# An mLSTM cell with a two-layer MLP: first-chunk gates loaded once and copied by TensorE, later masks by affine selections

## The chip, the cores and the metric

The kernel runs on one core of a Trainium2 chip. A core has five engines with queues of their own: TensorE (PE; its weight loads are shown as PEld), VectorE (DVE), ScalarE (ACT), GpSimd (POOL) and SyncE (SP), and 16 DMA engines that serve the loads and stores that the queues issue. Here SyncE and ScalarE issue them. The metric is the device time of one launch in microseconds, as the median of several runs; the time before is 476.22 us (three runs, 475.19 to 476.83).

## The reference

Four batches, eight heads, 768 steps, head dimension 40. Each step of the cell updates a matrix state `C` and a vector state `n` with stabilized gates; the result goes through a MLP with a leaky ReLU.

```python
for t in range(S):
    m_new = np.maximum(f[t] + m, i[t])
    f_stab = np.exp(f[t] + m - m_new)
    i_stab = np.exp(i[t] - m_new)
    m = m_new
    C = f_stab * C + i_stab * outer(v[t], k[t])
    n = f_stab * n + i_stab * k[t]
    y[t] = sigmoid(o[t]) * (C @ q[t]) / np.maximum(abs(n @ q[t]), 1.0)
...
x = y.transpose(0, 2, 1, 3).reshape(3072, 320)
h = x @ w_in            # 320 x 2048
out = np.maximum(0.01 * h, h) @ w_out   # 2048 x 320
```

The gates `i` and `f` are one number for each batch, head and step: 32 rows (batch times head) of 768.

## The kernel before

**Tiling.** The 768 steps are cut into six chunks of 128. A "step" `s` of the program is one batch of one chunk, `c, b = divmod(s, 4)`, so there are 24 of them. Within a chunk the cell is computed in parallel form: scores of keys and queries, multiplied by a matrix of exponentials of gate differences with a causal mask, times the values; the state is carried from chunk to chunk. Chunk 0 works on whole 128x128 score matrices; the later chunks use halves of 64. The MLP of a chunk (`ff_units`) is interleaved with the cell of the next one.

**Order.** The program order on TensorE, VectorE, ScalarE and GpSimd is written out by hand (`first_chunk`, then a loop over chunks); loads issued through `sync` or `by_act` keep their program order by the class `Ordered` (line 96 is the line of all SyncE issues). The weights come as 64-bit words and are turned into 32-bit floats on the chip by `narrow_weights` (two ScalarE and four VectorE instructions for each piece, lines 300 to 309).

**Gates of chunk 0.** Lines 109 to 111 load the first 128 columns of both gates four times each, into the four groups of 32 partitions of `f0` and `i0` (`RG` = 4), the forget gates by ScalarE's queue and the input gates by SyncE's. `gates(0)` then runs two scans and two subtractions on all 128 partitions (lines 325 to 333), which leaves `a` and `bu[:, 0]` four times. `a` lies in a corner of the buffer `acts` called `early`, beside the bf16 copies of the identity and of the causal mask. `gates(c)` for later chunks works on 32 partitions. `load_fi` loads the gates of later chunks; for chunks 1 and 2 ScalarE's queue issues them.

**The spread.** The matrix of exponents for a batch and head is mask[t', t] + bu[t'] + a[t]. `spread_masks` puts the mask into four PSUM banks by bf16 products (line 479). `spread_first` (line 495) adds the two others by products with a contraction of 32: one with a broadcast column of the identity as weights and `a` as moving operand, one the other way round with `bu`. The four products of a group of heads stand in the four groups of 32 rows, `rows = ts(r, BH)`, so TensorE can hold them side by side; this is what the four copies are for. `first_exps` (line 504, ScalarE) takes the exponentials for steps 0 and 1. A second spread, of `a` alone, serves steps 2 and 3.

**First-chunk order.** `first_chunk` (line 1169) issues the loads of steps 0 and 1 (keys, queries, values, then output gates), the first weights, then the gates, six products `warm(6)` whose result is never used (line 367), the mask products, the spread, the transposes of the gates (`gates_T`, lines 373 and 380), `prep_vu(0)` on GpSimd (lines 540 and 544), the exponentials, then `u_transpose(0)` (line 635: four transposes of the keys and four of the queries; the copies out of PSUM, line 638, are VectorE's here) and `u_scores(0)` (line 649 on TensorE, product with the exponentials on VectorE in line 653).

**Later masks.** In chunks 1 to 5, `spread(s)` or `feed_slowly` broadcasts `a` from a DRAM buffer into a tile `w` of 128 partitions x 8 heads x 64; partitions 0 to 63 and 64 to 127 hold the two halves of the chunk. `prep_mask` (line 522, GpSimd) adds `cm2`, the 64x64 causal mask in both halves of the partitions, which `prepare_tiles` copied into `i0` (line 176). `prep_exp` (line 530, ScalarE) takes the exponentials. `prep_mask` runs on GpSimd in one queue with `split_v` (line 413, values into their halves), the scaled state (line 684), the scaled keys (line 550) and others.

Of the kernel before, what the change touches and what calls it, by code (L numbers as in the profile page):

```python
# [8 lines left out]

F32 = mybir.dt.float32  # L10
# [4 lines left out]
ALU = mybir.AluOpType  # L15
# [4 lines left out]
def kernel(  # L20
# [26 lines left out]
    nc = tc.nc  # L47
    B, H, S, D = q.shape
    P = 128
    BH = B * H  # L50
# [11 lines left out]
    SL = P // 2  # L62
# [4 lines left out]
    GT = B * P  # L67
# [13 lines left out]
    wk = ctx.enter_context(tc.tile_pool(name="wk", bufs=2))  # L81
    psf = ctx.enter_context(tc.tile_pool(name="psf", bufs=4, space=PSUM))
    psc = ctx.enter_context(tc.tile_pool(name="psc", bufs=4, space=PSUM))
# [22 lines left out]
    i_all = i_gate.rearrange("b h s -> (b h) s")  # L106
    f0 = gp.tile([P, P], F32, name="f0")
    i0 = gp.tile([P, P], F32, name="i0")
    for r in range(RG):
        nc.scalar.dma_start(f0[ts(r, BH), :], f_all[:, :P])  # L110
        sync.dma_start(i0[ts(r, BH), :], i_all[:, :P])
    fi = {}

    def load_fi(c):
# [5 lines left out]
    load_fi(1)  # L120

    ident = consts.tile([P, P], F32, name="ident")
    make_identity(nc, ident[:])
    zeros = consts.tile([P, 1], F32, name="zeros")
    nc.vector.memset(zeros[:], 0.0)

# [4 lines left out]
        cmask[:], cmask[:], compare_op=ALU.is_ge, fill=-1e30,  # L131
        base=0, pattern=[[1, P]], channel_multiplier=-1,
    )
    cm2 = i0[:, :SL]

    NL = 4
# [8 lines left out]
    w_all = consts.tile([P, NL, H * P], F32, name="w")  # L147
    acts = consts.tile([P, NF, GT], F32, name="acts")
    acts_l = acts[:].rearrange("p f t -> p (f t)")
    early = acts_l[:, 5 * GT : 5 * GT + 3 * P].rearrange("p (n t) -> p n t", t=P)  # L150
    identb, cmaskb = (early[:, n, : P // 2].bitcast(BF16) for n in range(2))
    nc.gpsimd.tensor_copy(identb, ident[:])
    nc.gpsimd.tensor_copy(cmaskb, cmask[:])
    for n in range(NL):
        nc.vector.memset(kn[:, n, :, D:], 0.0)
        nc.vector.memset(qn[:, n, :, D:], 0.0)
        nc.gpsimd.memset(S_t[n][:, 1, :, D:], 2.0)
        nc.gpsimd.memset(S_t[n][SL:, 0], 0.0)
# [13 lines left out]

    def prepare_tiles():

        for u in range(2):
            nc.gpsimd.tensor_copy(cm2[ts(u, SL)], cmask[ts(u, SL), ts(u, SL)])
        nc.gpsimd.memset(xb[:], 0.0)
        for t in rb_t:
            nc.gpsimd.memset(t[:, :, RL:], 0.0)
# [138 lines left out]
    def gates(c):  # L318


        m0 = m0s.get(c)
        n = P if c == 0 else BH
        fc, il = (f0[:], i0[:]) if c == 0 else (fi[c][:, 0, :], fi[c][:, 1, :])
        F = wk.tile([n, P], F32, name="F", bufs=1)
        nc.vector.tensor_tensor_scan(F[:], fc, zeros[:n].to_broadcast([n, P]), 0.0, op0=ALU.add, op1=ALU.add)
        if c > 0:
            nc.vector.tensor_scalar(il, il, scalar1=m0[:], scalar2=None, op0=ALU.subtract)
        m = wk.tile([n, P], F32, name="m", bufs=1)
        nc.vector.tensor_tensor_scan(m[:], fc, il, -1e30 if c == 0 else 0.0, op0=ALU.add, op1=ALU.max)
        a = early[:, 2, :] if c == 0 else wk.tile([n, P], F32, name="a", bufs=1)  # L330
        nc.vector.tensor_tensor(a[:], F[:], m[:], op=ALU.subtract)
        bu = wk.tile([n, 3, P], F32, name="bu", bufs=1)
        nc.vector.tensor_tensor(bu[:, 0, :], il, F[:], op=ALU.subtract)
        if c + 1 < NB:
            m1 = wk.tile([BH, 1], F32, name="m0")
            if c == 0:
                nc.vector.tensor_copy(m1[:], m[:BH, P - 1 :])
            else:
                nc.vector.tensor_tensor(m1[:], m0[:], m[:, P - 1 :], op=ALU.add)
            m0s[c + 1] = m1  # L340
        if c > 0:
            na = wk.tile([BH, 1], F32, name="na")
            nc.vector.tensor_tensor(na[:], m[:, SL - 1 : SL], F[:, SL - 1 : SL], op=ALU.subtract)
        bus[c] = bu, a, (na if c > 0 else None)
# [19 lines left out]
    def warm(n):  # L364
        t = psf.tile([P, P], F32, name="warm", tag="mm")
        for _ in range(n):
            nc.tensor.matmul(t[:], lhsT=ident[:], rhs=ident[:], start=True, stop=True)
# [97 lines left out]
    def spread_q(s):  # L465
# [4 lines left out]
        for r in range(2):  # L470
            sync.dma_start(
                d["ea"][ts(r, SL)], a_dr[c, 1, 1 - r, b * H : (b + 1) * H, :].partition_broadcast(SL),
            )

    def spread_masks():

        ab = [psf.tile([P, 2, H // RG, P], F32, name=f"ab{r}", tag="mm") for r in range(RG)]
        for t in ab:
            nc.tensor.matmul(
                t[:].rearrange("p n m t -> p (n m) t"), lhsT=identb,  # L480
                rhs=cmaskb.unsqueeze(1).to_broadcast([P, 2 * H // RG, P]), start=True, stop=False, skip_group_check=True,
            )
        return ab

    def spread_first(ab, a, bu, s2):

        for n in range(2):
            st.setdefault(s2 + n, {})["w"] = w_all[:, s2 + n].rearrange("p (h t) -> p h t", t=P)
            for m in range(H // RG):
                for left in (False, True)[: 1 if bu is None else 2]:  # L490
                    for r in range(RG):
                        bh = (s2 + n) * H + m * RG + r
                        rows = ts(r, BH)
                        pick = ident[rows, r * BH + bh : r * BH + bh + 1].to_broadcast([BH, P])
                        nc.tensor.matmul(
                            ab[r][:, n, m, :], lhsT=bu[rows, 0, :] if left else pick, rhs=pick if left else a[rows, :],
                            start=False, stop=left or bu is None, skip_group_check=True,
                        )

# [17 lines left out]
    def prep_mask(s):  # L517
        if s in masked:
            return
        masked.add(s)  # L520
        w = st[s]["w"]
        nc.gpsimd.tensor_tensor(w, w, cm2.unsqueeze(1).to_broadcast([P, H, SL]), op=ALU.add)  # L522

    def prep_exp(s):

# [103 lines left out]
    def u_transpose(s, copies):  # L629
        d = st[s]  # L630
        d["kqT"] = wk.tile([P, 2, PR * P], F32, name="kqT")
        for i in range(2):
            tp = psc.tile([P, PR, P], F32, name="tkq", tag="c")
            for j in range(PR):
                nc.tensor.transpose(
                    tp[:, j, :], d["kq"[i]][:, 2 * j : 2 * j + 2, :].rearrange("p h d -> p (h d)"), ident[:],
                )
            copies[i](d["kqT"][:, i], tp[:].rearrange("p j t -> p (j t)"))
# [530 lines left out]
    def first_chunk():  # L1169

        for n in range(2):
            for i in range(3):
                load_first(n, i)
        for n in range(2):
            load_first(n, 3)
        load_weights(0, (0,))
        on_v, on_s = nc.vector.tensor_copy, nc.scalar.copy
        gates(0)
        gates_exp(0)
        load_fi(2)  # L1180
        warm(6)
        ab = spread_masks()
        bu, a, _ = bus[0]
        spread_first(ab, a, bu, 0)
        gates_T(0, bu)
        prep_vu(0)
        first_exps(ab, 0)
        u_transpose(0, (on_v, on_v))
        u_scores(0)
        u_transpose(1, (on_s, on_s))  # L1190
        ab = spread_masks()
        gates(1)
        u_scores(1)
        prep_vu(1)
        prepare_tiles()
        e = next_exps(ab, 2)
        w, w1 = narrow_weights(0, 0), narrow_weights(0, 1)
        n0, n1 = narrow_weights(1, 0), narrow_weights(1, 1)
        ffs = []
        prep_o(0)  # L1200
        prep_o(1)
        u_values(0)
        gate(0)
        spread_first(ab, a, None, 2)
        u_values(1)
        load_first(2, 0)
        load_first(2, 1)
        load_weights(0, (1,))
        load_first(3, 0)
        load_first(3, 1)  # L1210
        load_first(2, 2)
        load_first(3, 2)
        load_first(2, 3)
        load_first(3, 3)
        load_weights(1, (0,))
        load_weights(1, (1,))
        run(e, 6)
        u_x(0)
        gate(1)
        run(w, 2)  # L1220
        run(w, 4)
        u_x(1)
        state(0)
        state(1)
        state_copy(0)
        state_copy(1)
        prepare_step(0)
        prepare_step(1)
        run(e, 2)
        ffs = ff_units(0)  # L1230
        u_transpose(2, (on_s, on_s))
        run(e, 4)
        gates_exp(1)
        run(w1, 2)
        run(e, 4)
        ffs[0]()
        run(w1, 2)
        prep_vu(2)
        prep_vu(3)
        u_scores(2)  # L1240
        u_transpose(3, (on_v, on_s))
        run(w1, 2)
        u_gates(1)
        u_scores(3)
        prep_o(2)
        prep_o(3)
        u_values(2)
        ffs[1]()
        gate(2)
        u_values(3)  # L1250
        gate(3)
        u_x(2)
        state(2)
        u_x(3)
        state(3)
        state_copy(2)
        run(n0, 4)
        state_copy(3)
        run(n0, 2)
        run(n1, 6)  # L1260
        prepare_step(2)
        prepare_step(3)
        return ffs
# [160 lines left out]
```

## Time and profile before

| What | Value |
|---|---|
| median of three runs | 476.22 us |
| lowest and highest run | 475.19 and 476.83 us |
| span of the profiled execution | 472.6 us |
| TensorE busy | 462.6 us (98%) |
| TensorE weight loads busy | 417.8 us (88%) |
| VectorE busy | 339.1 us (72%) |
| ScalarE busy | 203.7 us (43%) |
| GpSimd busy | 172.0 us (36%) |
| mean granted TensorE clock | 0.999 |
| HBM traffic over the span | 124 GB/s |

The profile is one execution. The span runs from its first instruction to its last; the time of a run also holds what lies around the span. The views used below are: the chain of work that ended last, followed back from the end (the shares of the span that each engine or line holds in it; "SPq" is SyncE's queue issuing transfers); busy time by windows (for each engine the busy time and the number of instructions, then the granted clock, the busy share of the DMA engines and GB/s); the timeline (start, duration, engine, line, operation, tiles and shapes, a count where like instructions are merged, and in square brackets the idle time before it with what ended it); and the groups of instructions (busy time, mean ns of one, idle before). An f32 product of TensorE appears as two entries in the counts, a transpose as one.

### The profile page before, as it was taken

The numbers are of one execution on the slowest core, as the hardware profiler recorded it, in microseconds if no ns is written. First come the engines' busy times: TensorE is split into PE (matmuls) and PEld (weight loads), VectorE is DVE, ScalarE is ACT, GpSimd is POOL, SyncE is SP. The second block draws the span as 40 slices with busy tenths as digits, with TensorE's granted clock in tenths as the row PEclk, the third lists the DMA queues.
The fourth block names the chain that finished last, engine by engine and source line by source line (L and its number), as shares of the span: only waits on it lengthen the run. The fifth ranks groups of instructions, "written<-read, shape, count | busy, mean of one in ns | idle before, by whom it ended". The sixth has DMA issues, their size and how long they took to land.

```text
span 472.6 us, 14150 instructions
## 1 busy us (share of the span) xinstructions
PE 462.6 (98%) x5729; PEld 417.8 (88%) x5729; DVE 339.1 (72%) x607; ACT 203.7 (43%) x497; POOL 172.0 (36%) x205
## 2 busy tenths in 40 slices
PE   7998999999999999999999999999999999999997
PEld 6787878777788899988999988999988999988997
DVE  3878589999579989878688867788947786105531
ACT  3755888755336511367311366311456311253210
POOL 4340577264335164923214923214822005300020
PEclk9999999999999999999999999999999999999999
DMA  9999988877742594865755764853875203100001
GB/s 117 174 176 183 223 192 229 199 154 159 155 135 56 157 171 107 185 152 115 179 125 108 172 144 120 196 120 76 189 147 122 65 21 81 58 0 2 8 8 42
DMA packets 161281, 59.31 MB, mean 126 GB/s; under 512 B 123904, under 2 KB 152640, under 8 KB 161216
## 3 DMA queue, kind: packets, MB, share of 16 engines
q1 hardware_dynamic: 121088, 51.20, 49.0%
q10 hardware_dynamic: 40128, 7.21, 9.3%
q8 instruction: 45, 0.74, 0.7%
q14 instruction: 20, 0.16, 0.2%
HBM read 51.68 MB, written 6.70 MB: 124 GB/s over the span
## 4 chain that ended last, share of the span: by engine, by line
PE 86%; SPq 6%; DMA 3%; DVE 1%; ACT 1%; issue 1%; POOL 0%; DVEq 0%; ACTq 0%
PE ph L1021 33%; PE po L914 33%; PE po L879 8%; SPq L96 6%; PE pT L796 3%; PE sd L708 3%; PE ph L857 3%; DMA acts<-in_moe_w_in_dram 2%; DMA acts<-in_v_dram 1%; PE sd L714 1%; PE hN L768 1%; PE tk L621 0%; ACT kqT L627 0%; PE tq L606 0%; DVE w_in L308 0%
## 5 line engine op out<-in xcount | busy, mean ns | idle before, releaser
L914 PE MATMUL po<-w_out,acts 128*128 128x160 f32 x640 | 89.1, 300 | 0.0
L914 PEld LDWEIGHTS po<-w_out,acts 128*128 128x128 f32 x640 | 87.3, 190 | 0.6 <-ACT acts L1046 0.3
L1021 PE MATMUL ph<-xT,w_in 64*128 64x256 f32 x720 | 82.7, 378 | 0.0
L1021 PEld LDWEIGHTS ph<-xT,w_in 64*128 64x128 f32 x720 | 69.5, 187 | 8.3 <-issue 0.6
L1050 DVE TENSOR_TENSOR acts<-acts,ph 128x512 f32<-128x512 f32 x60 | 38.4, 682 | 40.4 <-PE ph L1021 40.3
L914 PE MATMUL po<-raw,acts 128*128 128x160 f32 x480 | 66.4, 300 | 0.0
L914 PEld LDWEIGHTS po<-raw,acts 128*128 128x128 f32 x480 | 65.4, 190 | 0.3
L1054 ACT COPY acts<-ph 128x512 f32<-128x512 f32 x60 | 32.2, 588 | 49.5 <-PE ph L1021 49.5
L522 POOL TENSOR_TENSOR w<-w,i 128x512 f32<-128x512 f32 x20 | 31.9, 1603 | 53.2 <-DMA w<-a_dr 22.1
L1046 ACT ACTIVATE acts<-acts 128x1024 f32<-128x1024 f32 x30 | 31.6, 1055 | 40.6 <-DVE acts L1050 32.3
L684 POOL TENSOR_TENSOR S<-S,f 40x336 f32<-40x336 f32 x36 | 31.3, 868 | 46.7 <-PE pT L796 31.1
L530 ACT ACTIVATE w<-w,gT 128x64 f32<-128x64 f32 x160 | 41.6, 337 | 12.3 <-DMA a_dr<-a 5.3
L725 DVE TENSOR_TENSOR qn<-w,sd 64x384 f32<-64x384 f32 (+1 forms) x80 | 33.4, 418 | 13.7 <-ACT acts L1054 7.8
L857 PE MATMUL ph<-xT,w_in 64*128 64x256 f32 x320 | 37.9, 383 | 1.8 <-DVE w_in L309 0.7
L879 PE MATMUL po<-w_out,acts 128*128 128x320 f32 x128 | 36.7, 437 | 0.0
L857 PEld LDWEIGHTS ph<-xT,w_in 64*128 64x128 f32 x320 | 31.5, 187 | 5.8 <-ACT acts L865 1.1
L810 POOL TENSOR_TENSOR xb<-xb,den 128x320 f32<-128x320 f32 x16 | 11.6, 727 | 67.7 <-DVE xb L807 65.4
L1021 PE MATMUL ph<-acts,w 64*128 64x256 f32 x320 | 36.3, 379 | 0.0
L1021 PEld LDWEIGHTS ph<-acts,w 64*128 64x128 f32 x320 | 30.6, 187 | 3.6
L879 PEld LDWEIGHTS po<-w_out,acts 128*128 128x128 f32 x128 | 23.5, 190 | 9.2 <-ACT acts L865 0.3
L595 DVE TENSOR_TENSOR qn<-kqT,ea 64x512 f32<-64x512 f32 x32 | 30.9, 965 | 0.8
L952 POOL TENSOR_TENSOR y<-y,raw 128x160 f32<-128x160 f32 x10 | 9.5, 953 | 59.2 <-ACT y L951 59.2
(181 smaller groups left out, 736.5 us busy)
## 6 DMA issues: line engine op xcount, KB each, us to landing
rb<-in_k_dram SPq DMA_DIRECT2D x64, 80.0 KB
rb<-in_q_dram SPq DMA_DIRECT2D x64, 80.0 KB
rb<-in_o_gate_dram SPq DMA_DIRECT2D x64, 80.0 KB
ea<-a_dr SPq DMA_DIRECT2D x32, 128.0 KB
raw<-in_moe_w_out_dram SPq DMA_DIRECT2D x6, 640.0 KB
w<-a_dr ACTq DMA_DIRECT2D x24, 128.0 KB
x_dr<-x SPq DMA_DIRECT2D x64, 40.0 KB
xT<-x_dr SPq DMA_DIRECT2D x16, 160.0 KB
```

The lines of the kernel that those rows point to most:

```text
L522: nc.gpsimd.tensor_tensor(w, w, cm2.unsqueeze(1).to_broadcast([P, H, SL]), op=ALU.add)
L530: yield nc.scalar.activation(w[:, h, :], w[:, h, :], AF.Exp, bias=gT[c][:, 0, bh : bh + 1], scale=1.0)
L595: nc.vector.tensor_tensor(mixed(s)[rows, 1 - r], d["kqT"][rows, 1].rearrange("p (h t) -> p h t", t=SL), d["ea"][rows], op=ALU.mult,)
L684: nc.gpsimd.tensor_tensor(new, old, g, op=ALU.mult)
L725: nc.vector.tensor_tensor(mixed(s)[toks, u, hs], w[toks, hs], bank[1 - u][to[u][hs.start], hs], op=ALU.mult,)
L857: nc.tensor.matmul(ph[r][:, cols], lhsT=w_row(r, slot, j), rhs=xT[DP * r : DP * (r + 1), slot, cols], start=(slot == 0), stop=(slot == KC ...
L879: nc.tensor.matmul(po[n][:], lhsT=acts[:, f, ts(n, P)], rhs=w_out[:, f, :], start=(f == 0), stop=(f == NF - 1),)
L914: nc.tensor.matmul(bank[:], lhsT=left[:, f, :], rhs=right[:, f, :], start=f == 0, stop=f == KH - 1)
L1021: nc.tensor.matmul(bank[r][:, e, :], lhsT=left(r)[rows, e], rhs=right(r)[rows], start=first and e == 0 and m == 0, stop=e == 1 and m == le ...
L1046: nc.scalar.activation(to, z, AF.Prelu, alpha=0.01)
L1050: nc.vector.tensor_tensor(to[:, 2 * r : 2 * r + 2], to[:, 2 * r : 2 * r + 2], bank[r], op=ALU.add)
L1054: nc.scalar.copy(to[:, 2 * r : 2 * r + 2], bank[r])
```

## The change

- Each gate of chunk 0 is loaded once, into 32 partitions; `gates(0)` works on 32 partitions, with `a` in a tile of its own.
- A new function `replicate` makes the four copies: a matrix of 32 x 128 that holds the 32x32 identity four times (`early[:BH, 2]`, written by GpSimd) is the weight of two products with `a` and `bu[:, 0]`; VectorE copies the result of 128 x 256 from PSUM to `early`. `spread_first` takes its operands from there.
- `u_transpose(0)` is moved ahead of `spread_first`, behind `replicate`.
- `warm(6)` becomes `warm(2)`.
- The identity is built by a memset and two selections of 64x64 on its diagonal, instead of `make_identity`, which was a memset and one selection of 128x128.
- `prep_mask` no longer adds a mask tile: two affine selections on GpSimd, one for each half of the partitions, fill -1e30 where the column is before the row. `cm2` and the two copies that built it are gone.

```diff
-    for r in range(RG):
-        nc.scalar.dma_start(f0[ts(r, BH), :], f_all[:, :P])
-        sync.dma_start(i0[ts(r, BH), :], i_all[:, :P])
+    nc.scalar.dma_start(f0[:BH], f_all[:, :P])
+    sync.dma_start(i0[:BH], i_all[:, :P])
...
-    make_identity(nc, ident[:])
+    nc.gpsimd.memset(ident[:], 0.0)
+    for u in range(2):
+        part = ident[ts(u, SL), ts(u, SL)]
+        nc.gpsimd.affine_select(
+            part, part, compare_op=ALU.not_equal, fill=1.0, base=0, pattern=[[-1, SL]], channel_multiplier=1,
+        )
...
-    cm2 = i0[:, :SL]
...
-    early = acts_l[:, 5 * GT : 5 * GT + 3 * P].rearrange("p (n t) -> p n t", t=P)
+    early = acts_l[:, 5 * GT : 6 * GT].rearrange("p (n t) -> p n t", t=P)
...
+    nc.gpsimd.tensor_copy(early[:BH, 2, :].rearrange("p (r n) -> p r n", r=RG), ident[:BH, :BH].unsqueeze(1).to_broadcast([BH, RG, BH]))
...
-        for u in range(2):
-            nc.gpsimd.tensor_copy(cm2[ts(u, SL)], cmask[ts(u, SL), ts(u, SL)])
...
-        n = P if c == 0 else BH
-        fc, il = (f0[:], i0[:]) if c == 0 else (fi[c][:, 0, :], fi[c][:, 1, :])
+        n = BH
+        fc, il = (f0[:BH], i0[:BH]) if c == 0 else (fi[c][:, 0, :], fi[c][:, 1, :])
...
-        a = early[:, 2, :] if c == 0 else wk.tile([n, P], F32, name="a", bufs=1)
+        a = wk.tile([n, P], F32, name="a", bufs=1)
...
+    def replicate(a, bu):
+
+        rows = early[:, 2:]
+        t = psc.tile([P, 2, P], F32, name="rep", tag="c")
+        pick = rows[:BH, 0, :]
+        for n, part in enumerate((a[:], bu[:, 0, :])):
+            nc.tensor.matmul(t[:, n, :], lhsT=pick, rhs=part, start=True, stop=True)
+        nc.vector.tensor_copy(rows, t[:])
+        return rows[:, 0, :], rows[:, 1, :]
...
-        nc.gpsimd.tensor_tensor(w, w, cm2.unsqueeze(1).to_broadcast([P, H, SL]), op=ALU.add)
+        for u in range(2):
+            part = w[ts(u, SL)]
+            nc.gpsimd.affine_select(
+                part, part, compare_op=ALU.is_ge, fill=-1e30, base=0, pattern=[[0, H], [1, SL]], channel_multiplier=-1,
+            )
...
-        warm(6)
+        warm(2)
         ab = spread_masks()
         bu, a, _ = bus[0]
-        spread_first(ab, a, bu, 0)
+        a, left = replicate(a, bu)
+        u_transpose(0, (on_v, on_v))
+        spread_first(ab, a, left, 0)
         gates_T(0, bu)
         prep_vu(0)
         first_exps(ab, 0)
-        u_transpose(0, (on_v, on_v))
         u_scores(0)
```

More of the change, by code (lines that the diff above doesn't have):

```diff
@@ L6 @@
 from concourse.bass import ts
-from concourse.masks import make_identity
 from concourse._compat import with_exitstack
@@ L336, in gates @@
             if c == 0:
-                nc.vector.tensor_copy(m1[:], m[:BH, P - 1 :])
+                nc.vector.tensor_copy(m1[:], m[:, P - 1 :])
             else:
@@ L495, in spread_first @@
                         nc.tensor.matmul(
-                            ab[r][:, n, m, :], lhsT=bu[rows, 0, :] if left else pick, rhs=pick if left else a[rows, :],
+                            ab[r][:, n, m, :], lhsT=bu[rows, :] if left else pick, rhs=pick if left else a[rows, :],
                             start=False, stop=left or bu is None, skip_group_check=True,
```

## The prediction

> **What bounds the kernel.** I read the shares of the chain first, then busy time by window, then the timeline of the first 20 us and of 36 to 72 us, and last who waited for whom there.
>
> ```profile
> PE 86%; SPq 6%; DMA 3%; DVE 1%; ACT 1%; issue 1%; POOL 0%; DVEq 0%; ACTq 0%
> ...
> 126.00:200.00 74.00, 74.00 (x1040) 69.21 (x1040) 61.35 (x101) 27.58 (x71) 38.99 (x35) 1.00 0.62 135
> ```
>
> The second line is a stretch of 74 us in which TensorE is busy for 74.00. The windows from 70 to 400 us are all like it, so nothing that shortens VectorE or GpSimd work there can shorten the run. TensorE is busy 462.6 of 472.6 us; most of the 10 us that are open lie before 70 us, and before 52 us the chain is not TensorE's. It is SyncE's row of DMA issues, unbroken from 0.75 to 28.96 us, then a transfer of 8.66 us:
>
> ```profile
> 28.96 8.66 DMA acts<-in_moe_w_in_dram
> ...
> 37.73 0.80 ACT w_in L300
> ```
>
> So the run is a head paced by transfers, behind which about 400 us of full TensorE lie. What the head gains or loses by 70 us appears at the end nearly whole.
>
> ```profile
> 0.75 1.79 SPq L96 DMA_DIRECT2D i<-in_i_gate_dram  x4
> 0.76 1.84 ACTq L110 DMA_DIRECT2D f<-in_f_gate_dram  x4
> 2.58 0.42 SPq L96 DMA_DIRECT2D kn<-in_k_dram  x1
> 4.03 0.42 DVE L325 TENSOR_TENSOR_SCAN F<-f,zeros 128x128 f32<-128x128 f32 x1 [1.47 <-DMA f<-in_f_gate_dram]
> 6.03 0.81 PE L495 MATMUL ab<-acts,ident 32*128 32x128 f32 x8
> 8.43 0.39 PE L495 MATMUL ab<-ident,bu 32*128 32x128 f32 x8
> 8.83 0.66 PE L635 MATMUL tkq<-ident,kn 128*128 128x128 f32 x4
> 10.87 1.16 PE L649 MATMUL sc<-kqT 40*128 40x128 f32 x16 [0.94 <-DVE kqT L638]
> 12.13 1.28 DVE L653 TENSOR_TENSOR w<-w,sc 128x512 f32<-128x512 f32 x2 [1.32 <-PE sc L649]
> ```
>
> Four issues on each queue come ahead of everything else. The scan of the gates waits for the last f piece, and the keys cannot be asked for before 2.58.
>
> ```profile
> 3.00:4.00 1.00, 1.00 (x7) 1.00 (x7) 0.00 (x0) 0.33 (x1) 0.89 (x3) 1.00 0.38 71
> 4.00:5.00 1.00, 1.00 (x4) 0.43 (x4) 0.94 (x3) 0.95 (x1) 0.89 (x3) 1.00 1.09 199
> ```
>
> The last two columns are the busy share of the transfer engines and GB/s: 0.38 and 71 in the fourth microsecond, 1.09 and 199 in the fifth. Until the keys are asked for the engines are mostly empty; afterwards they are behind, since the same kind of 160 KB load takes 0.42 us to issue at 2.58 but 1.16 at 5.19.
>
> **Three loads fewer on each queue.** Four issues on SyncE take 1.79 plus the gap to 2.58, so 0.46 each. Three fewer bring the keys and all loads behind them 1.38 us forward (2.58 to 1.20). The bytes that vanish (6 x 16 KB = 98 KB) moved while the engines were mostly idle, and I count nothing for them. The Trainium skill, DMA: Bandwidth & Descriptors, section "Issuing engines are not separate DMA queues", says that the time a sequencer takes to initiate a transfer is usually small relative to the transfer. By that rule only bytes would count, an estimate of 98 KB at the 180 GB/s of the later windows, 0.5 us; the row at 71 GB/s speaks for the issue time here.
>
> The stream keeps the 1.38 us as long as it stays behind. The signs that it does, up to 63 us:
>
> ```profile
> 37.73 0.79 ACT L300 ACTIVATE w_in<-acts 128x640 f32<-128x640 f32 x1 [0.37 <-DMA acts<-in_moe_w_in_dram]
> ...
> 45.42 0.80 ACT L300 ACTIVATE w_in<-raw 128x640 f32<-128x640 f32 x1 [2.17 <-DMA raw<-in_moe_w_in_dram]
> ...
> 46.05 0.25 PE L621 MATMUL tk<-ident,kn 64*40 64x64 f32 x2 [1.07 <-DMA kn<-in_k_dram]
> ...
> 60.93 1.79 POOL L522 TENSOR_TENSOR w<-w,i 128x512 f32<-128x512 f32 x1 [7.27 <-DMA w<-a_dr]
> 62.97 0.95 POOL L413 COPY S<-acts 64x320 f32<-64x320 f32 x2 [0.24 <-DMA acts<-in_v_dram]
> ...
> 69.64 0.23 PE L714 MATMUL sd<-S,vu 64*40 64x42 f32 x1 [0.96 <-POOL vu L550]
> ```
>
> At each of them the last wait ends with a transfer or with GpSimd work right behind one. For the whole shift to reach 37.73, compute must be earlier by about 1.0 (1.38 less the 0.37 that ScalarE idled); at 45.42 ScalarE has 2.17 to spare, and the transfer alone decides.
>
> **The compute of the head.** The scan now starts 1.43 us after the last f issue ends (2.60 to 4.03). One issue ends at 1.22, so it starts at 2.65; the memsets of VectorE end at 2.56 and do not hold it. Its five instructions take 1.32 (4.03 to 5.35) and end at 3.97, 1.38 earlier.
>
> GpSimd ahead of TensorE: one 128x128 selection (0.29) becomes two of 64x64. None of that size is in the trace; a 64x64 copy is 0.23 and the whole selection 0.29, so I take 0.27 each, +0.25. The bf16 masks are ready at 2.4 instead of 2.13. The copy of the picks (at most the 0.29 of a 128x128 copy) ends at 2.7. GpSimd's queue behind it, eight memsets ending at 5.58, moves by 0.5; its next work comes at 9.41, so nobody waits.
>
> TensorE: warm products go from 12 entries to 4, at 0.22 each 1.7 to 2.6. The mask products (4.19 to 6.03, 1.84) then run 2.6 to 4.45. The two copying products stand in the same 32 rows and cannot lie side by side as a group of eight L495 entries does in 0.41; 2 x 0.41 gives 5.3. The VectorE copy of 128x256 lies between 0.22 (128x64, L380) and 0.65 (128x512, L638): 0.38, ready at 5.75. Meanwhile the eight transposes of step 0 run: 1.1 us at the fast pace (8.83 to 9.93), twice that at the slow one; I take 1.7, to 7.0. They need q of step 0. By the bytes per microsecond the first 480 KB were in by 5.7, and 1.38 earlier with a microsecond to land is 5.3, when only k is being transposed; if q came 1 us later, the spread would too.
>
> The spread's eight groups take 0.41 each at the start and 0.22 from 7.5 on: 1.8 at best, 3.3 at worst. From 7.0 with the pace rising as before: 8.9. Exponentials start 9.2 instead of 8.85, 0.35 later. But the scores of step 0 no longer wait for the copies of kqT (VectorE makes these from 6.2 to 7.7, ahead of its copy of gT): they end by 10.3 instead of 12.03. The product L653 then waits for the exponentials, 11.3 for its second half, and ends at 11.95 against 13.41. Compute gains 1.4 (0.2 with the slow pace throughout, 1.8 with the fast one), enough for the 1.0 above. The transposes of step 1 and the copies that fill kqT on ScalarE move by as much.
>
> **Masks.** Twenty sums of 128x512 become forty selections of 64x512; the two 64x64 copies that made the mask (0.52, at 12.80) go.
>
> ```profile
> 1.37 0.29 POOL L130 TENSOR_SCALAR_AFFINE_SELECT cmask<-cmask 128x128 f32<-128x128 f32 x1
> ...
> 2.39 0.52 POOL L158 MEMSET S<- 64x512 f32 x1
> ...
> L522 POOL TENSOR_TENSOR w<-w,i 128x512 f32<-128x512 f32 x20 | 31.9, 1603 | 53.2 <-DMA w<-a_dr 22.1
> ```
>
> No selection of 512 columns is in the trace. From below: the memset's slope, (0.52 - 0.20)/384 = 0.83 ns per column, on 0.29 gives 0.61. From above: four times 0.29 is 1.16. A pair is 1.2 to 2.3 against 1.60. A selection has one input like the memset, so I take 1.3. From 70 us on TensorE covers either end. Before, two places can feel it. The first mask (48.77 to 50.49) ends just ahead of the exponentials at 51.12, after a gap of 0.43 on ScalarE, whose L865 releases TensorE at 52.41 (idle 0.73): 0.3 gained, or 0.6 lost. The second ends at 62.72, 0.24 ahead of a transfer: nothing gained, or 0.5 lost before the GpSimd chain that TensorE awaits at 69.64. The transfer behind the second takes back most of what the first gains: I count 0.05, with -0.6 and +0.7 as ends.
>
> **Sum.** 1.38 + 0.05 = 1.4 us. Span 472.6 becomes 471.2. The median of the runs is 3.6 above that span; 476.22 - 1.4 = 474.8.
>
> **Rivals.** (B) Only part arrives: the slow pace leaves compute 0.2 earlier, so 0.2 + 0.37 = 0.6 reaches 37.73, VectorE, unbroken from 38.55 to 54, holds it there, slow selections take 0.6 back, or only the removed bytes count (98 KB at 199 GB/s, 0.5 us). 475.6. The issue rule above would end here. For it: VectorE and ScalarE are full from 15 to 28 us. Against: the idle 2.17 and 1.07 at 45 and 46.
>
> (C) Slower: TensorE's pace rises too late. Before, it doubles near 7.3 us after nearly unbroken work, eight warm products among it, while the granted clock reads 1.00 throughout. The Trainium skill, TensorE: Matmul & The Clock Gate, Part 4 (PE-mode transpose), says that transposes don't count as busy for the gate; that speaks against putting them here. No row shows transposes ahead of a rise. If the pace rises only after 13 us, the spread ends at 10.3, scores 0 at 12.6 (2 x 1.0), transposes 1 at 14.3, mask products at 16.0, where scores 1 started at 13.85: 2.15 late, less 0.37, so 1.8 lost: 478.0. A rise near 10.7 would only give B; it turns into a loss from there on. Against: the pace held through the transposes at 8.83, and TensorE's row is again nearly unbroken.
>
> (D) More: the smaller GpSimd load also frees VectorE, whose L302 at 49.29 took 1.56 beside L522 and 0.49 at 42.54. Then the idle 0.73 and 0.96 of TensorE at 52.41 and 69.64 close as well: 1.4 + 1.7 = 3.1, 473.1. Against: both are fed by other work too.
>
> **Chances.** Forecast 0.45, B 0.23, C 0.12, D 0.20. What a measurement of this kernel can tell from no change is about 0.3%, 1.43 us, so below 474.8 counts as faster. The forecast sits on that bound and is halved. Faster: 0.225 + 0.20 = 0.43. Slower, above 477.6: most of C, 0.10. Same: 0.47. The range leaves out C and the end of D: 473.2 to 476.8; the forecast's own is 474.2 to 475.4.
>
> **What would show it.** The first key load at 1.20, the scan at 2.65, scores 0 right behind the gate transposes without an idle; L300 near 36.35 and 44.0; TensorE's last wait near 68.2; selections of 0.6 to 0.7. Wrong would be a last TensorE wait still near 69.6, spread groups of 0.41 beyond 9 us, or selections over 0.9.

## The result, and the profile after

The median of eight runs is 473.65 us (473.05 to 474.58). Eight runs of the kernel before have a median of 475.47 us. The ratio is 0.9961 with a 95% interval of 0.9947 to 0.9975, so the change saves 1.8 us (1.2 to 2.5). The forecast was 1.4 us.

The profiled execution after has a span of 472.2 us and a time of 473.96 us, 1.8 apart. The prediction took 3.6 us between span and time from the profile before; that execution (span 472.6, so about 474.4 us by the same 1.8) was quicker than all eight runs of its kernel (474.64 and up), so the two profiles stand closer together than the two kernels do. In the chain that ended last, SyncE's issues have lost their place at the start:

```profile
PE 89%; SPq 4%; ACT 3%; POOL 2%; DMA 1%; issue 1%; DVE 0%; POOLq 0%
```

Followed back, this chain runs over TensorE and ScalarE up to 35.3 us and over SyncE's queue from 35.71. Loads and compute come out of the head close together: in the run of the masks alone below, which has the old head, the chain is also compute up to 29.6 us. So which of the two leads differs from one execution to the next.

The timeline of the head (start, duration, engine, line, shapes, idle before):

```profile
1.19 0.42 SPq L95 DMA_DIRECT2D kn<-in_k_dram  x1
...
2.59 0.41 DVE L325 TENSOR_TENSOR_SCAN F<-f,zeros 32x128 f32<-32x128 f32 x1
...
7.61 0.81 PE L505 MATMUL ab<-acts,ident 32*128 32x128 f32 x8
...
9.48 0.58 PE L505 MATMUL ab<-acts,ident 32*128 32x128 f32 x8
9.89 0.39 PE L505 MATMUL ab<-ident,acts 32*128 32x128 f32 x8
...
12.37 1.29 DVE L667 TENSOR_TENSOR w<-w,sc 128x512 f32<-128x512 f32 x2 [1.19 <-ACT w L514]
```

The keys are asked for at 1.19 instead of 2.58 and the scan starts at 2.59 instead of 4.03, as worked out. But the spread (L505, L495 before) starts at 7.61 instead of 6.03, keeps the slow pace until 9.7, and the first product of scores and exponentials (L667, L653 before) runs at 12.37 instead of 12.13: all of the early start of compute is gone. The windows of the fourth and fifth microsecond, last two columns the busy share of the DMA engines and GB/s, show the other half:

```profile
3.00:4.00 1.00, 1.00 (x3) 0.30 (x2) 0.86 (x5) 0.69 (x2) 0.89 (x3) 1.00 1.12 178
4.00:5.00 1.00, 1.00 (x4) 0.43 (x3) 0.00 (x0) 0.27 (x1) 0.89 (x3) 1.00 1.42 175
```

178 GB/s flow in the fourth microsecond, where 71 did. What becomes of this at the waits named in the prediction:

```profile
37.26 0.80 ACT L300 ACTIVATE w_in<-acts 128x640 f32<-128x640 f32 x1
...
44.04 0.79 ACT L300 ACTIVATE w_in<-raw 128x640 f32<-128x640 f32 x1 [1.26 <-DMA raw<-in_moe_w_in_dram]
...
62.35 0.94 POOL L413 COPY S<-acts 64x320 f32<-64x320 f32 x2 [0.42 <-DMA acts<-in_v_dram]
...
69.01 0.23 PE L728 MATMUL sd<-S,vu 64*40 64x42 f32 x1 [1.14 <-POOL vu L564]
```

At 37.26 ScalarE has no wait any more (0.37 for a transfer before): compute decides there, and only 0.47 us are gained. At 44.04 (45.42 before) the transfer decides again and the whole 1.38 us are there. That it agrees to 0.01 is luck: the same wait ends at 44.15 in the run with six unused products below, and with the head alone the weights are there by 43.19. At 62.35 (62.97) and 69.01 (69.64) this profile keeps 0.6 of them.

### The profile page after: what moved, and what is told of

Read it like the earlier page. It is cut to its first block, busy times and chain, and to the rows that moved or that the text cites. A ratio compares the mean times of both kernels' runs of the same rounds, so it can differ in the third digit from the quotient of the medians.

```text
span 472.2 us, 14183 instructions
## 1 busy us (share of the span) xinstructions
PE 463.5 (98%) x5725; PEld 417.6 (88%) x5725; DVE 340.0 (72%) x608; ACT 203.1 (43%) x497; POOL 171.4 (36%) x225
## 4 chain that ended last, share of the span: by engine, by line
PE 89%; SPq 4%; ACT 3%; POOL 2%; DMA 1%; issue 1%; DVE 0%; POOLq 0%
PE ph L1035 33%; PE po L928 33%; PE po L893 8%; SPq L95 4%; PE pT L810 3%; PE sd L722 3%; PE ph L871 2%; DMA w<-a_dr 1%; ACT w L523 1%; PE sd L728 1%; PE ab L505 1%; PE hN L782 1%; PE pa L757 1%; PE sc L663 0%; PE tk L635 0%
## 5 line engine op out<-in xcount | busy, mean ns | idle before, releaser
L534 POOL TENSOR_SCALAR_AFFINE_SELECT w<-w 64x512 f32<-64x512 f32 x40 | 33.7, 844 | 53.3 <-DMA w<-a_dr 52.1
L698 POOL TENSOR_TENSOR S<-S,f 40x336 f32<-40x336 f32 x36 | 30.2, 840 | 48.4 <-PE pT L810 32.9
```

The source lines that it names most:

```text
L534: nc.gpsimd.affine_select(part, part, compare_op=ALU.is_ge, fill=-1e30, base=0, pattern=[[0, H], [1, SL]], channel_multiplier=-1,)
L698: nc.gpsimd.tensor_tensor(new, old, g, op=ALU.mult)
```

## The experiments

Theory S is the prediction's: the gain is SyncE's stream of loads, which starts 1.38 us earlier. Rivals: the masks (M), and compute in the head. Each run has its median over 12 executions if no other number is given, and the ratio to runs of the kernel before on the same chip, with its 95% interval.

**Masks alone.**

```diff
# the kernel before
-        nc.gpsimd.tensor_tensor(w, w, cm2.unsqueeze(1).to_broadcast([P, H, SL]), op=ALU.add)
+        for u in range(2):
+            part = w[ts(u, SL)]
+            nc.gpsimd.affine_select(part, part, compare_op=ALU.is_ge, fill=-1e30, ...)
```

> The kernel before, with the later masks by affine selections and nothing else of the change. Theory S (the gain is the stream of loads that starts 1.38 us earlier): no change, ratio to the kernel before 0.999 to 1.001, the last wait of TensorE near 69.6 us as before. Rival M (smaller GpSimd work at 47 to 70 us frees VectorE and ScalarE): 1 us or more faster, ratio 0.998 or less, last wait of TensorE before 69.0.

Measured: 475.15 us, ratio 0.9991 (0.9976 to 1.0007). No difference that can be told.

**The head alone.**

```diff
# the changed kernel
-        for u in range(2):
-            part = w[ts(u, SL)]
-            nc.gpsimd.affine_select(part, part, compare_op=ALU.is_ge, fill=-1e30, ...)
+        nc.gpsimd.tensor_tensor(w, w, cm2.unsqueeze(1).to_broadcast([P, H, SL]), op=ALU.add)
```

> The changed kernel, with the later masks added from a mask tile as before; the head is the changed one. Theory S: as fast as the changed kernel, ratio to the kernel before 0.996, ScalarE's wait for the first half of the third weight block ends near 44.0 us. Rival M: most of the gain is gone, ratio 0.998 to 1.0.

Measured over 10 executions: 473.52 us, ratio 0.9960 (0.9942 to 0.9977), the whole change. These two runs are halves of one comparison, and each was profiled in one of its quickest executions, so their timelines can be laid side by side. Masks alone, with the old head (lines are shifted by the edits):

```profile
45.61 0.79 ACT L297 ACTIVATE w_in<-raw 128x640 f32<-128x640 f32 x1 [2.29 <-DMA raw<-in_moe_w_in_dram]
...
63.32 0.94 POOL L410 COPY S<-acts 64x320 f32<-64x320 f32 x2 [1.09 <-DMA acts<-in_v_dram]
...
69.98 0.23 PE L715 MATMUL sd<-S,vu 64*40 64x42 f32 x1 [1.04 <-POOL vu L551]
```

The head alone, with the old masks:

```profile
43.19 0.81 ACT L303 ACTIVATE w_in<-raw 128x640 f32<-128x640 f32 x1
...
61.84 0.95 POOL L416 COPY S<-acts 64x320 f32<-64x320 f32 x2 [0.53 <-DMA acts<-in_v_dram]
...
68.51 0.23 PE L727 MATMUL sd<-S,vu 64*40 64x42 f32 x1 [1.14 <-POOL vu L563]
```

The values that GpSimd waits for land 1.48 us earlier, TensorE's last wait ends 1.47 earlier, and the spans are 472.8 and 471.3. Between these two profiles, a lead as large as that of the keys (2.58 to 1.20) reaches the end. It isn't the transfer's at every place: at 43.19 ScalarE no longer waits for the weights.

**Three issues put back ahead of the keys.** The rows they fill are read by nothing.

```diff
     sync.dma_start(i0[:BH], i_all[:, :P])
+    for r in range(1, RG):
+        sync.dma_start(i0[ts(r, BH), :], i_all[:, :P])
```

> The changed kernel, with three more loads of the input gates (16 KB each, into rows that nothing reads) on SyncE's queue ahead of the keys, so that the keys are issued at 2.58 us again; all compute is as in the changed kernel. Theory S: it loses 1.4 us, ratio to the kernel before 0.999, and the wait at 44.0 us returns to 45.4. Rival (the gain comes from compute in the head or from the masks): ratio 0.996 still.

Measured: 475.68 us, ratio 1.0007 (0.9991 to 1.0023). The whole gain is gone, although the rest of the change is in place. Its timeline:

```profile
2.58 0.43 SPq L95 DMA_DIRECT2D kn<-in_k_dram  x1
...
7.58 1.11 PE L651 MATMUL tkq<-ident,qn 128*128 128x128 f32 x4 [0.69 <-DMA qn<-in_q_dram]
...
13.34 1.29 DVE L669 TENSOR_TENSOR w<-w,sc 128x512 f32<-128x512 f32 x2 [1.19 <-ACT w L516]
...
45.52 0.79 ACT L302 ACTIVATE w_in<-raw 128x640 f32<-128x640 f32 x1 [1.76 <-DMA raw<-in_moe_w_in_dram]
```

The wait of 44.04 is back at 45.52. The loss is more than 1.4 us, and there is a second cost in it: the transposes of step 0, now ahead of the spread, wait 0.69 for the queries, and the product of scores and exponentials moves from 12.37 to 13.34. The next run tells the two apart. The three loads bring 48 KB back too, 0.3 us at the 180 GB/s of the prediction; the loss is several times that.

**Transposes of step 0 back behind the exponentials.**

```diff
         a, left = replicate(a, bu)
-        u_transpose(0, (on_v, on_v))
         spread_first(ab, a, left, 0)
...
         first_exps(ab, 0)
+        u_transpose(0, (on_v, on_v))
```

> The changed kernel, with the transposes of step 0 behind the exponentials of the spread as before. Theory S: time as the changed kernel within 0.3 us (ratio 0.995 to 0.997), as transfers decide at 44 us. Rival on the late pace: the transposes ahead of the spread hold TensorE slow until 9.7 us; with the spread in their place its groups reach 0.22 us by 8 us, as in the kernel before. If the pace is slow until 9.7 here too, the transposes are not its cause (the shorter warming or the window's phase would be).

Measured: 474.13 us, ratio 0.9971 (0.9955 to 0.9987), at the edge of what was expected; the interval includes the changed kernel's 0.9961. All but the last group of its spread run at the slow pace, until 9.5 us, with no transposes ahead of them, and the product comes at 13.41:

```profile
9.10 0.65 PE L505 MATMUL ab<-acts,ident 32*128 32x128 f32 x8
9.52 0.57 PE L505 MATMUL ab<-ident,acts 32*128 32x128 f32 x8
...
13.41 1.28 DVE L667 TENSOR_TENSOR w<-w,sc 128x512 f32<-128x512 f32 x2 [1.32 <-PE sc L663]
```

So the late pace doesn't need the transposes ahead of it. And this run, beside the one before it on the same chip, settles the rival of compute in the head: the product comes equally late in both (13.34 and 13.41, against 12.13 in the kernel before), but the keys are asked for at 2.58 in the one and at 1.20 in the other, and the medians are 475.68 and 474.13 us. With compute later than in the kernel before, the larger part of the gain is still there.

**Six unused products instead of two.**

```diff
-        warm(2)
+        warm(6)
```

> The changed kernel, with six unused products at the start instead of two. Theory on the pace (TensorE's pace follows its full-array work in the first microseconds, and the shorter warming moved its rise from 7.2 to 9.7 us): groups of the spread at 0.22 us from about 7.5 us on, the mask products end near 6.2 and the spread near 10.2, so the end of the spread hardly moves; time within 0.4 us of the changed kernel. If the pace rises at 9.7 or later all the same, the transposes or the 32-row products are its cause.

Measured: 473.65 us, ratio 0.9961 (0.9949 to 0.9973). In its profile the pace is fast from 5.9 us on, earlier than the 7.5 expected, and the product of scores and exponentials runs at 11.23, 1.1 us earlier than in the changed kernel. The median is the changed kernel's: within the interval of 0.6 us to either side, this microsecond of compute gains nothing. ScalarE waits 2.17 us for the weights again, until 44.15. On the pace, the count over all profiles speaks for the theory without showing it: with six unused products it rose between 5.2 and 7.3 us (four profiles), with two between 9.1 and 10.9 in nine and at 5.2 in one.

**Both gates issued by ScalarE's queue**, so that SyncE starts with the keys; alone, and with six unused products.

```diff
-    sync.dma_start(i0[:BH], i_all[:, :P])
+    nc.scalar.dma_start(i0[:BH], i_all[:, :P])
```

> The changed kernel, with the one load of the input gates issued by ScalarE's queue behind that of the forget gates, so that the keys are the first issue of SyncE, 0.45 us earlier still. Theory S with the stream alone: 0.3 to 0.45 us faster than the changed kernel, ratio to the kernel before 0.995. If compute is the limit by now (TensorE idled only 0.33 for the keys at 44.1 us): no gain over the changed kernel, ratio 0.996.

> Both edits together: input gates by ScalarE's queue, six unused products. If stream and compute each hold back what the other gains, this one is faster than either alone, 0.4 us or more below the changed kernel; if only the stream counts, it equals the one with the gates by ScalarE's queue.

Measured: 474.11 us, ratio 0.9970 (0.9958 to 0.9982) alone, 473.88 us over 7 executions and 0.9963 (0.9948 to 0.9979) with the products. Neither beats the changed kernel; a gain of 0.45 us, or a loss as small, lies within the intervals. The keys do start at 0.75, but the 16 KB of input gates, issued at 1.25 beside them, hold the second scan until 5.51 (2.93 in the changed kernel), and the product of scores and exponentials is 1.5 us later (13.84). TensorE no longer waits for the keys of step 4 in this profile, ScalarE no longer for the weights (44.92), so compute decides at these places.

**The three extra loads behind the loads of steps 0 and 1**, where the DMA engines are behind anyway.

```diff
             load_first(n, 3)
+        for r in range(1, RG):
+            sync.dma_start(i0[ts(r, BH), :], i_all[:, :P])
         load_weights(0, (0,))
```

> The changed kernel, with the same three extra loads of 16 KB on SyncE's queue as in the run that put them ahead of the keys, but behind the loads of steps 0 and 1, where the DMA engines are behind anyway. If issue time counts only while the engines are empty: no loss but for 48 KB (0.3 us), ratio to the kernel before 0.996 to 0.997. If each issue costs its 0.45 us wherever it stands in the queue: 1.4 us or more lost, ratio 0.999 or more.

Measured: 474.81 us, ratio 0.9995 (0.9981 to 1.0009). That issue time counts only while the engines are empty was not borne out: 0.3 us was expected for that case. The three small loads hold the queue for 2.79 us (0.76, 0.42 and 1.51), and the weights behind them start at 12.06 instead of 9.22:

```profile
9.22 2.79 SPq L95 DMA_DIRECT2D i<-in_i_gate_dram  x3
12.06 2.03 SPq L95 DMA_DIRECT2D acts<-in_moe_w_in_dram  x3
```

Part of this loss is a second effect that the windows of the same execution show (TensorE busy is the third number, the granted clock is third from the end):

```profile
22.00:23.00 1.00, 0.00 (x0) 0.00 (x0) 0.95 (x3) 0.26 (x1) 0.00 (x0) 0.58 1.37 160
...
25.00:26.00 1.00, 1.00 (x6) 0.74 (x6) 0.00 (x0) 1.00 (x6) 0.00 (x0) 0.50 0.15 24
...
29.00:30.00 1.00, 1.00 (x16) 0.88 (x15) 0.14 (x1) 0.57 (x3) 0.85 (x3) 1.00 1.45 189
```

TensorE idled 1.60 us for ScalarE up to 21.01 and 1.49 for the queries of step 2 from 21.64 to 23.13. Its granted clock fell to 0.50 within the second idle, at about 22.2 (an estimate from the 0.58 of that window), and stayed there until 29. Four of the 12 executions have a mean clock below 0.998; the eight others have a median of 474.5 us, still 0.85 above the changed kernel.

**Issues or bytes?** Three variants of the same place, and one that merges loads. One load of 48 KB instead of three of 16:

```diff
+        sync.dma_start(i0[BH:, :], i_gate.rearrange("b h (c s) -> (b h c) s", s=P)[: P - BH, :])
```

> The changed kernel, with one extra load of 48 KB (96 rows of 512 bytes, into rows that nothing reads) behind the loads of steps 0 and 1 on SyncE's queue, where three loads of 16 KB cost about 1.3 us. If the cost is by issue: 0.45 us or less lost against the changed kernel, ratio to the kernel before 0.997 or less. If it is by bytes or rows: the same 1.3 us, ratio 0.999.

Three loads of 1 KB:

```diff
+        for r in range(1, RG):
+            sync.dma_start(i0[ts(r, BH), :8], i_all[:, :8])
```

> The changed kernel, with three extra loads of 1 KB (32 rows of 32 bytes) at that place. If the cost is by issue: 1.3 us lost, ratio 0.999. If it is by bytes: nothing lost, ratio 0.996.

Steps 2 and 3 in merged loads (`load_pair` issues one load for both steps):

```diff
-        load_first(2, 0)
-        load_first(2, 1)
+        load_pair(2, 0)
+        load_pair(2, 1)
         load_weights(0, (1,))
-        load_first(3, 0)
-        load_first(3, 1)
...
-        load_first(2, 3)
-        load_first(3, 3)
+        load_pair(2, 3)
```

> The changed kernel, with the loads of steps 2 and 3 merged in pairs (keys, queries and output gates of both steps in one load each: three issues fewer on SyncE's queue, same bytes and descriptors, keys and queries of step 3 ahead of the second half of the first weight block). If the cost is by issue: 0.4 us a piece, about 1.3 us faster than the changed kernel, ratio 0.993. If it is by bytes or descriptors: as the changed kernel, ratio 0.996.

The three loads of 16 KB by ScalarE's queue near 5 us:

```diff
         load_fi(2)
+        for r in range(1, RG):
+            nc.scalar.dma_start(i0[ts(r, BH), :], i_all[:, :P])
```

> The changed kernel, with the three extra loads of 16 KB issued by ScalarE's queue while it is idle, near 5 us. If SyncE's queue alone is what counts: no loss, ratio 0.996. If the DMA engines lose the time whoever issues: 1 us or more lost, ratio 0.998 to 0.999.

Measured, in that order: 475.49 us, 0.9975 (0.9952 to 0.9998); 476.05 us, 0.9984 (0.9963 to 1.0006); 475.55 us, 0.9970 (0.9948 to 0.9993); 475.40 us, 0.9972 (0.9946 to 0.9998). On this chip the runs of the kernel before scatter from 475.16 to 481.06 us, and the intervals are wider; all four overlap the changed kernel's. So the first, the second and the fourth run can't tell their two outcomes apart. In issue time the one large load (first fence) and the three tiny ones (second) differ less than their bytes:

```profile
9.12 1.15 SPq L95 DMA_DIRECT2D i<-in_i_gate_dram  x1
```

```profile
9.30 1.66 SPq L95 DMA_DIRECT2D i<-in_i_gate_dram  x3
```

Two of the 1 KB loads take about 0.42 us each and one 0.73. The 0.42 is also what 16 KB (0.40) and 160 KB (0.42) took in SyncE's first three microseconds, so at its shortest an issue there takes about 0.4 us, whatever its size. Where the engines are behind it can take longer: 48 KB take 1.15 in one load and 2.79 in three. Neither issues nor bytes alone fit. What of it arrives at the end stays open. The merged loads save issues, but their second weights are issued at 16.36 instead of 12.57, and 9 of 12 executions have a mean clock below 0.998 (4 of 12 in the run with issues later); the gain of 1.3 us that the count of issues would give isn't there: its ratio of 0.993 lies outside the interval. No version tried beats the changed kernel.

## Why the prediction came out right

**Three loads fewer** was sized 1.38 us and measured 1.39 at the keys (2.58 to 1.19) and 1.38 at the weights (45.42 to 44.04; 44.0 was forecast). The two half-changes agree that it arrives at TensorE's last wait (1.47 between their profiles). That the issues ahead of the keys cause the gain is shown by putting them back (ratio 1.0007), beside the run in which compute is as late but the keys are not (0.9971). The forecast 68.2 for the last wait was 69.01 in the changed kernel's profile, 68.51 with the old masks; single executions differ by that much.

**Why the issue time counts** was only half understood. The prediction tied it to engines that stand idle in the fourth microsecond; the same loads put where the engines are behind still cost 0.85 us in the executions without a dip, about half of the gain. The rule of the Trainium skill weighed there (DMA: Bandwidth & Descriptors, "Issuing engines are not separate DMA queues") says that initiating is usually small beside the transfer. The prediction's estimate from it was a gain of 0.5 us; 1.8 (1.2 to 2.5) came, so this case doesn't agree.

**The compute of the head** is the step that failed: 1.4 us earlier was forecast, 0.2 with the slow pace throughout; 0.25 later came (the product ends at 13.66 instead of 13.41). Two terms were too small. The spread started at 7.61 instead of 7.0: the two copying products took 1.15 us where 0.85 was counted, the transposes 1.89 where 1.7 was. And its pace, taken "as before" to rise near 7.3 us, rose at 9.7, so that the spread took until 10.45 instead of 8.9. So the row forecast for 36.35 came at 37.26, near what rival B gave for that place (0.6 gained; 0.47 came). The time didn't follow B, because 44.04 has its own transfer to wait for. For the time this was nearly a spare condition: with compute 1.1 us earlier than in the changed kernel the median is the same, with compute 1.0 us later it is 474.13.

Of the three signs of being wrong, the spread groups of 0.41 us beyond 9 us came, and they marked this step. The last wait, 69.01, lies between the 68.2 of the forecast and the 69.6 of the sign; the selections stayed under 0.9 us in the mean.

**Rival C** had the right symptom with the wrong cause. The late pace came, but it comes without transposes ahead of it too, and with them the rise came at 5.2 us in the run with later issues. The change also left out four of the six unused products (six with twelve entries, not the "eight" of the prediction); that this delays the rise is likelier by the count above, but not shown. So the Trainium skill's sentence on transposes (TensorE: Matmul & The Clock Gate, Part 4) decides nothing here. Its Part 1, by which the window runs free, so that the rise depends on where in it a kernel starts, fits better: two kernels with the same TensorE program up to the scores rose at 5.2 and 9.7. But these lie 4.5 us apart, and the Trainium skill gives 0.5 us to either side there.

**Masks** were counted at 0.05 us, and no difference can be told (0.9991). The selection itself came as worked out where nothing disturbs it, 656 ns at the median for 650 forecast, but not in the sum:

```profile
L534 POOL TENSOR_SCALAR_AFFINE_SELECT w<-w 64x512 f32<-64x512 f32 x40 | 33.7, 844 | 53.3 <-DMA w<-a_dr 52.1
```

33.7 us against 31.9 for the sums. The wrong term is the comparison: 1.3 for a pair is an undisturbed price, and the 1.60 of a sum was a mean with everything that disturbed it, one record of 5.58 us among it. An undisturbed sum takes 1.27 us (the median of the twenty), so a pair of selections is no smaller. The mean of a pair, 1.69, holds one record of 4.68 us in turn. Rival D had VectorE freed: L302 near 49.3 did fall from 1.56 to 1.00 us (the 0.49 that the prediction gives for it at 42.54 is L305's; L302 took 0.48 at 42.02). But TensorE's two idles, which D would close, are 0.89 and 1.14 instead of 0.73 and 0.96.

**The absolute time**, 474.8, was too high by 1.15: 0.75 because the median of the first three runs (476.22) stood above that of eight, 0.4 because the gain was 1.8 rather than 1.4. The chances had the forecast on the bound of 0.3%, and it fell on the faster side.

## What to carry to other kernels

Where a head is paced by one queue of loads, count the issues ahead of the first load that matters, and price each at its issue time, not its bytes; a copy that another engine can make is worth it even if it delays compute a little, as long as compute has slack at the next transfer. Price an old and a new instruction alike, both undisturbed or both by their means. Judge a change of 0.3% by medians over many runs, by pairs of half-changes, and by pairs of runs in which only one of two paths is late: one profile of each kernel showed a third of this gain at the last wait. Costing work on TensorE in its first ten microseconds needs both paces as bounds.

## What the runs showed of the hardware

- TensorE's pace in the head doubled between 5.2 and 10.9 us, at 5.2 and at 9.7 with the same TensorE program, with a granted clock of 1.00 in the record throughout.
- After an idle of 1.6 us and about 0.5 us into the next, the granted clock fell to 0.50 for 6.8 us (about 22.2 to 29.0). In the profile of the merged loads it fell at about 30.3 for as long, after 1.2 us of idle in the three microseconds before. Executions of the kernel with later issues that have a mean clock below 0.998 have a median 1.6 us above the others (476.1 and 474.5).
- A load of 16 KB issued 0.5 us behind the first keys, on another queue, let its reader start only 4.3 us after its issue (1.25 to 5.51). Issued first, at 0.75, its reader started at 2.93.
- The issue of a load in the head took 0.39 to 0.42 us of SyncE's queue at its shortest, for 1, 16 and 160 KB alike. Where the engines were behind, it took up to 0.73 (1 KB) and 1.51 us (16 KB).
